# Placing seven heads' attention output by 48 small products, and the FFN's first products in two column groups, in a one-core decode layer

## The chip, the cores and the metric

The kernel runs on one core of a Trainium2 chip. The metric is the device time of one execution in microseconds. Only the core's own engines matter: TensorE (PE, with its weight loads PEld), VectorE (DVE), ScalarE (ACT), GpSimd (POOL), SyncE (SP), and the 16 DMA engines that its queues feed.

## What is computed

One token (D = 448) goes through a layer norm, and then through two branches that are added to x:

```python
xn = _layernorm(x)
# A: 16 query heads on 8 key/value heads, 65536 keys of 256 numbers each, cached in HBM
q = (xn @ wq)                                  # 448 x 4096
p = softmax(q k^T * 256 ** -0.5)               # for each head over 65536 keys
A = (p @ v).reshape(1, 4096) @ wo              # 4096 x 448
# B: a gated FFN on the same row, scaled by sigmoid(xn . w_r)
y = (silu(xn @ w_gate) * (xn @ w_up)) @ w_down # 448 x 1792, 448 x 1792, 1792 x 448
B = xn + sigmoid(xn . w_r) * y
out = x + A + B
```

All inputs are bfloat16. The key and value caches are 268 MB each; with the weights some 549 MB are read once.

## The kernel before, in words

The keys and values of one kv head are cut into four turns, 32 turns in all. One turn's keys (8 MB) land in one of two ring slots, its values (8 MB) in the third slot. In a turn PE transposes the keys (fp32 pairs of bf16) into `ps_t`, DVE and ACT copy them to `kt_all`, PE forms the scores (`k_QK`, into `ps_q`), ACT copies them out (`EVQ`), PE turns them round (`k_JT`, into `ps_s`), then come the maximum (`pe_m1t`), its broadcast (`pe_bc`), the exponentials on ACT (`EXP`), their sum (`pe_tot`, copied by DVE as `LS`), and one turn later the product with the values (`pe_V`, four column groups into `ps_o`), its transposition (`dve_ob`, `pe_oT`) into `oT_all`. Each engine runs its own list in the order in which the program writes it; a `W` is a semaphore wait of one engine, an `O` an operation that others can wait for. SP issues all large loads in one queue, in the order of the `item` calls.

The change touches the end (`ending`), which runs after the last turn's key sets. Seven of the eight heads are complete by then but for the scaling of their four turns against each other; the last head still lacks its last turn, whose values are the last large load. Before, PE and DVE worked in this order:

1. `pe_turn`: DVE scales and adds the seven heads (`head_weights`, `OTF`), PE transposes the result (`OTROW`), DVE writes it as 14 rows of 256 (`OROW`), and ACT's queue stores it to HBM (`hop 0`, tensor `o_flat`) and, once it has landed, loads it back as 128 partitions of 28 numbers (`hop 1`, tile `oT_h`). Partition p then holds the inputs 28p to 28p+27 of `wo`, whose rows lie in SBUF in the same order (`wo_rows`).
2. the last turn's maximum, `BC`, exponentials and `TOT`, and the weights of the last head.
3. `pe_ffn1`: 2 x 14 products of 448 columns for gate and up, into four PSUM banks; ACT's sigmoid (`SG`), DVE's two multiplications (`GS`, `H`); `pe_ffn_hT`: 14 small products that put the 1792 numbers on partitions (`HTP`, copied as `HTH`); `pe_ffn2`: 14 products with `w_down`.
4. `pe_attn`: 16 of the 28 columns of `oT_h` times their rows of `wo`, into one row of `ps_q`; DVE adds FFN, residual and this row (`YS`, `YX`, `SUM`).
5. `FIN_BASE` puts that sum into `ps_s` as the start of an accumulation in two column groups (`fin`: columns 0 to 207 and 208 to 447, on partitions 0 and 32). Then the last values: `pe_V` in two parts of 48 and 16 products (the program's main block ends between them), `dve_ob`, `pe_oT`, the other 12 columns of `oT_h` (`FIN_X`), the last head (`FIN`), two copies and the store of the output.

The last loads in SP's queue are the last values in two parts (6 MB and 2 MB), `wo` rows in two parts (`wx`, 896 and 448 KB) and the last head's `wo` rows in three parts (`wo_end`). These three go into a part of `kt_all` and wait for `HT`, that is for `HTH`.

Of the kernel before, what the change touches and what calls it, by code (L numbers as in the profile page):

```python
# [21 lines left out]
def bass_parallel_sum__gqa_block_cached__moe_arch_mod__decode_kernel(  # L22
# [625 lines left out]

    def pe_turn():
        W("dve", "OTSB", NU - 2)  # L650
        head_weights(0, Hkv - 1, 0, NT)
        for hf in range(NH):
            W("dve", "OW", 0, hf)
            O("dve", ("OTF", hf), lambda it, hf=hf: nc.vector.tensor_reduce(
                out=oT_f[:, hf, :, :], in_=oT_all[:, hf, 1:1 + NT, :].rearrange("p (h t) i -> p h i t", t=U), axis=AX.X, op=ALU.add))
# [12 lines left out]

    def hop(k, dst, src):
        items["oh", k] = ("oh%d" % k, 16)  # L670
        prog["act"].append(("d", here[0], ("DMA", "oh", k), (dst, src), "oh%d" % k))

    def pe_attn():
        W("pe", "DMA", ("oh", 1))
        W_item("pe", "wo")
        O("pe", "ATTN", lambda it: [mm(ps_a, lhsT=oT_h[:, f:f + 1], rhs=wo_all[:, f * D:(f + 1) * D],
                                       start=f == 0, stop=f == FR - WX - 1) for f in range(FR - WX)][-1])

    def pe_ffn1():
# [16 lines left out]

        O("pe", "FFN1G", half(0, 0))
        for c in range(2):
            W("act", "FFN1G")
            O("act", ("SG", c), lambda it, c=c: nc.scalar.activation(out=sg_sb[c], in_=ps_tf[c][0:2, 0:FB], func=ACTF.Sigmoid))  # L700
        O("pe", "FFN1", half(WGN // 2, 2))
        v = nc.vector
        for c in range(2):
            W("dve", "SG", c)
            O("dve", ("GS", c), lambda it, c=c: v.tensor_tensor(out=sg_sb[c], in0=ps_tf[c][0:2, 0:FB], in1=sg_sb[c], op=ALU.mult))
        for c in range(2):
            W("dve", "GS", c)
# [1 line left out]
            O("dve", ("H", c), lambda it, c=c: v.tensor_tensor(out=h_sb[:, c * FB:(c + 1) * FB], in0=sg_sb[c],
                                                               in1=ps_tf[2 + c][0:2, 0:FB], op=ALU.mult))  # L710

    def pe_ffn_hT():
        W("pe", "H", 0)
        W("pe", "H", 1)
        W("pe", "LS", NU - 1)

        def f(it):
            hv = h_sb.rearrange("s (p t) -> s p t", t=FK)
            for t in range(FK):
                ins = mm(ps_m[0:P // 2, C_HT + 2 * t:C_HT + 2 * t + 2], lhsT=hv[:, :, t],  # L720
                         rhs=sel_bf[0:2, 0, :], start=True, stop=True)
# [4 lines left out]
        for k in range(2):  # L726
            O("dve", ("HTH", k), lambda it, k=k: nc.vector.tensor_copy(
                out=hT_sb[k * P // 2:(k + 1) * P // 2, :],
                in_=ps_m[0:P // 2, C_HT:C_HT + 2 * FK].rearrange("p (t s) -> p s t", s=2)[:, k, :]))
# [46 lines left out]
    def ending():  # L776
# [4 lines left out]
        k_QK(n - 1)  # L781
        pe_turn()
        k_JT(n - 1)
        W("pe", "OROW")
# [4 lines left out]
        pe_tot(T)
        head_weights(Hkv - 1, Hkv, NT, NU - 1)  # L790
        for hf in range(NH):
            W("dve", "OW", Hkv - 1, hf)
            O("dve", ("OTE", hf), lambda it, hf=hf: nc.vector.tensor_reduce(
                out=oT_e[:, hf, :], in_=oT_all[:, hf, 1 + NT:NU, :].rearrange("p t i -> p i t"), axis=AX.X, op=ALU.add))
# [16 lines left out]
        O("dve", "SUM", lambda it: nc.vector.tensor_tensor(out=sum_f, in0=ps_a, in1=sum_f, op=ALU.add))
# [308 lines left out]
```

## Time and profile before

| | |
|---|---|
| median of 3 runs | 1285.49 us (1284.19 to 1285.6) |
| the profiled execution, its time | 1284.63 us |
| its span, first to last instruction | 1283.3 us |
| busy: PE, DVE, ACT | 73%, 45%, 36% of the span |
| bytes read from HBM | 549.04 MB, 428 GB/s over the span |
| mean granted TensorE clock | 0.867 |

In the rows of the timeline the first number is the start and the second the length, both in microseconds of the span; what stands in brackets is how long the engine had been idle and what released it. Each line of the table of stretches gives busy time and, after x, the number of instructions of each engine, then the granted clock (1.00 is full, 0.50 half), the share of the time that the DMA engines moved data, and GB/s. A DMA row ends in the time from issue to landing. PE's products all carry one line number, that of a helper, so they are told apart by their tiles: output, then what they read.

### The profile page before, as it was taken

To read this page: it belongs to the slowest core of one execution; us is meant where nothing else is said; L and a number is where in the kernel's file an instruction comes from. 1 tells how busy PE (TensorE), PEld (TensorE's weight loads), DVE (VectorE), ACT (ScalarE), POOL (GpSimd) and SP (SyncE) were. 2 spreads that over 40 slices of the span, in tenths; PEclk is the share of its full clock that TensorE was granted. 3 is DMA by queue.
4 is the path that set the end of the run, shared out by engine and by line. 5 is a ranking of instruction groups with operands and counts; after the bars stand their busy time and mean duration, and the time that the engine had idled before them with its cause. 6 is when DMAs were issued, how large, how long until landed. Compare 5 with 4: busy or idle time off the path is not lost. (4 is left out here: it accounts for less than half of the span.)

```text
span 1283.3 us, 23437 instructions
## 1 busy us (share of the span) xinstructions
PE 938.5 (73%) x9761; PEld 646.4 (50%) x9761; DVE 576.8 (45%) x1123; ACT 462.8 (36%) x719; POOL 8.0 (1%) x37
## 2 busy tenths in 40 slices
PE   1887877678866777876678867668766668766677
PEld 1655655445644445654455544445544445544453
DVE  2554544435543445444345444345444345444352
ACT  0543433334432334333234333334333334333330
POOL 2000000000000000000000000000000000000000
PEclk9998978888887889888789878899888889888898
DMA  9999999999999999999999999999999999999995
GB/s 408 435 439 427 433 437 435 427 435 437 435 425 437 435 435 429 433 441 429 429 437 439 427 433 435 437 427 437 435 435 427 435 437 433 429 437 439 427 425 244
DMA packets 10990, 549.19 MB, mean 428 GB/s; under 512 B 1362, under 2 KB 1764, under 8 KB 2020
## 3 DMA queue, kind: packets, MB, share of 16 engines
q1 hardware_dynamic: 10804, 549.03, 99.0%
q8 instruction: 7, 0.11, 0.0%
q10 hardware_dynamic: 176, 0.02, 0.0%
q14 instruction: 3, 0.02, 0.0%
HBM read 549.04 MB, written 0.01 MB: 428 GB/s over the span
## 5 line engine op out<-in xcount | busy, mean ns | idle before, releaser
L404 PE MATMUL ps_t<-ident_f,ring 128*128 128x128 f32 x4096 | 627.4, 298 | 311.1 <-DMA ring<-in_A_k_cache_dram 277.8
L465 DVE COPY kt_all<-ps_t 128x1024 bf16<-128x1024 bf16 x768 | 492.2, 685 | 584.0 <-PE ps_q L404 574.2
L404 PEld LDWEIGHTS ps_t<-ident_f,ring 128*128 128x128 f32 x4096 | 485.5, 151 | 472.6 <-DMA ring<-in_A_k_cache_dram 280.6
L467 ACT ACTIVATE kt_all<-ps_t 128x1024 bf16<-128x1024 bf16 x256 | 262.3, 1025 | 411.1 <-PE ps_q L404 410.8
L404 PE MATMUL ps_q<-kt_all,q_cur 128*2 128x512 bf16 x2056 | 175.3, 419 | 5.4 <-ACT s L489 5.0
L467 ACT ACT_TABLE_LOAD x32 | 41.1, 1283 | 362.7 <-PE ps_q L404 362.7
L489 ACT ACTIVATE s<-ps_q 98x512 bf16<-98x512 f32 x257 | 151.6, 590 | 1.3 <-PE ps_q L404 1.3
L404 PE MATMUL ps_o<-ring,p_sb 128*4 128x512 bf16 x2048 | 117.7, 382 | 0.3 <-PEq L1075 0.3
L404 PEld LDWEIGHTS ps_o<-ring,p_sb 128*4 128x4 bf16 x2048 | 46.0, 85 | 57.0 <-issue 3.5
L404 PEld LDWEIGHTS ps_s<-sel_bf,s 128*128 128x128 bf16 x1032 | 62.7, 98 | 3.8 <-ACT s L489 0.6
L404 PE MATMUL ps_s<-sel_bf,s 128*128 128x8 bf16 x1032 | 63.7, 167 | 0.5 <-ACT s L489 0.5
L588 DVE CAST ob_sb<-ps_o 100x512 bf16<-100x512 f32 x33 | 22.8, 691 | 90.2 <-PE ps_o L404 90.2
L404 PEld LDWEIGHTS ps_q<-kt_all,q_cur 128*2 128x2 bf16 x2056 | 26.8, 79 | 56.9 <-issue 44.4
L549 ACT ACTIVATE p_sb<-S_sb,negmax 128x128 bf16<-128x128 bf16 x66 | 26.8, 428 | 5.4 <-DVE negmax L541 5.4
L404 PEld LDWEIGHTS ps_m<-diag,ones_f 2*128 2x128 f32 x66 | 9.9, 186 | 10.3 <-DVE diag L532 10.3
L404 PE MATMUL ps_m<-diag,ones_f 2*128 2x2 f32 x66 | 12.7, 260 | 2.4 <-DVE diag L532 0.6
L520 DVE TENSOR_REDUCE m<-S_sb 128x2 f32<-128x256 bf16 x33 | 13.9, 420 | 1.1
L517 DVE CAST S_sb<-ps_s 128x256 bf16<-128x256 f32 x33 | 13.7, 415 | 0.0
L549 ACT ACTIVATION_READ_ACCUMULATOR p_sb<-S_sb,negmax 128x1 f32 x66 | 12.4, 188 | 0.0
L404 PEld LDWEIGHTS ps_m<-rowsum,ones_f 128*128 128x128 f32 x66 | 10.2, 195 | 1.3 <-DVE gm_all L543 1.3
L404 PE MATMUL ps_m<-rowsum,ones_f 128*128 128x2 f32 x66 | 9.6, 215 | 1.3 <-ACT p_sb L549 1.3
L404 PE MATMUL ps_m<-ident_f,m 128*2 128x128 f32 x33 | 9.1, 276 | 1.3 <-DVE m L520 1.3
(98 smaller groups left out, 131.5 us busy)
## 6 DMA issues: line engine op xcount, KB each, us to landing
ring<-in_A_v_cache_dram SPq DMA_DIRECT2D x1, 6144.0 KB, 22.7
ring<-in_A_wq_dram SPq DMA_DIRECT2D x1, 3584.0 KB, 11.2
ring<-in_A_v_cache_dram SPq DMA_DIRECT2D x1, 2048.0 KB, 27.3
ring<-in_A_wo_dram SPq DMA_DIRECT2D x1, 1792.0 KB, 42.6
ring<-in_B_w_gate_dram SPq DMA_DIRECT2D x1, 1568.0 KB, 32.5
ring<-in_B_w_up_dram SPq DMA_DIRECT2D x1, 1568.0 KB, 35.9
ring<-in_B_w_down_dram SPq DMA_DIRECT2D x1, 1568.0 KB
ring<-in_A_wo_dram SPq DMA_DIRECT2D x1, 896.0 KB, 29.1
```

What stands on the lines that cost most here:

```text
L404: return pe.matmul(*a, **k)
L465: O(e, ("EV", s, m), lambda it: nc.vector.tensor_copy(out=kt[:, :], in_=tb[:, :]), f"ev{m}")
L467: O(e, ("EV", s, m), lambda it: nc.scalar.activation(out=kt[:, :], in_=tb[:, :], func=ACTF.Copy), f"ev{m}")
L489: O("act", ("EVQ", s), lambda it: nc.scalar.activation(out=s2[s % 2][0:QROWS, :], in_=ps_q[0:QROWS, :], func=ACTF.Copy), "evq")
L517: O("dve", ("SCOPY", u), lambda it: nc.vector.tensor_copy(out=S_sb[:, :, :], in_=ps_sn), "sc")
L520: O("dve", ("M1", u), lambda it: nc.vector.tensor_reduce(out=m1[:, :], in_=S_sb[:, :, :].rearrange("p n i -> p i n"), axis=AX.X, op=ALU.max))
L549: O("act", ("EXP", b, i), lambda it, i=i: nc.scalar.activation(out=p_sb[:, :, i], in_=S_sb[:, :, i], func=ACTF.Exp, bias=negmax[:, i:i + 1 ...
L588: O("dve", ("OB", t), lambda it: nc.vector.tensor_copy(out=ob_sb[0:OROWS, :], in_=ps_o[0:OROWS, :]))
```

## The change

The way through HBM goes. DVE converts the seven heads' sums to bf16 (`OTG`, tile `oT_g`), and 48 products with columns of the identity matrix as weights (32 columns each, in four column groups, one to three result columns) place them in PSUM (`pe_rows`, into `ps_q`), from where DVE copies them to `oT_h` (`OTH`). For this the rows of `wo` lie in another order: partition p of a pair of kv heads holds 8 neighbouring rows of that pair, and of the seventh head 4. The first load of `wo` (two pairs, 1792 KB) so has two stretches of 7168 bytes on each partition, not one of 14336; the late ones keep theirs. The identity matrix gets a tile of its own, since its old place is overwritten by values.

`pe_ffn1` alternates its products between two column groups (partitions 0 and 32) of one bank for the gate and one for up. It moves ahead of the last turn's maximum: the new order on PE is FFN1, the 48 products, M1T, `HTP` (now into `ps_o`), BC, FFN2, TOT, `FIN_BASE`, ATTN, the last values. ATTN now adds into `ps_s` in two column groups (32 products in place of 16), behind `FIN_BASE`; the operation `SUM` is gone. On DVE `OTH` stands ahead of `GS` and `H`, and `LS` and the last head's weights behind `HTH`. On ACT the sigmoids stand ahead of the last exponentials.

```diff
-    ident_bf = slots[2][:, SLOT - P:SLOT]
+    ident_bf = S_("ident_bf", [P, P], BF16)
...
     def wo_rows(f0, f1):
-        return A_wo[0:(Hq - rep) * Dh, :].rearrange("(p f) n -> p f n", f=FR)[:, f0:f1, :].rearrange("p f n -> p (f n)")
+        r = A_wo[f0 * P:f1 * P, :]
+        if f1 <= PR * NPAIR:
+            return r.rearrange("(k p c) n -> p k (c n)", p=P, c=PR)
+        return r.rearrange("(k p c) n -> p k (c n)", k=1, p=P)
...
-        for hf in range(NH):
-            W("pe", "OTF", hf)
-            O("pe", ("OTROW", hf), ...)
-        W("dve", "OTROW", NH - 1)
-        O("dve", "OROW", ...)
-        W("act", "OROW")
-        hop(0, o_flat, o_row)
+        W("dve", "OTF", NH - 1)
+        O("dve", "OTG", lambda it: nc.vector.tensor_copy(out=oT_g[:, :, :, :], in_=oT_f[:, :, :, :]))
+
+    def pe_rows():
+        W("pe", "OTG")
+        W("pe", "EVQ", NU * SETS - 1)
+        def f(it):
+            for a in range(PR // NH):
+                for hf in range(NH):
+                    for g in range(NG):
+                        o = ps_r[32 * g:32 * g + 32, 0:PR * NPAIR].rearrange("p (k c) -> p c k", c=PR)[:, a * NH + hf, :]
+                        mm(o, lhsT=ident_bf[:, a:P:PR // NH], rhs=oT_g[:, hf, g // rep:2 * NPAIR:2, g % rep],
+                           start=True, stop=True, tile_position=(0, 32 * g))
+            ...  # 16 more for the seventh head, one result column each
+        O("pe", "OROW", f)
+        W("dve", "OROW")
+        O("dve", "OTH", lambda it: nc.vector.tensor_copy(out=oT_h[:, :], in_=ps_r))
...
     def pe_attn():
-        W("pe", "DMA", ("oh", 1))
         W_item("pe", "wo")
-        O("pe", "ATTN", ... mm(ps_a, lhsT=oT_h[:, f:f + 1], rhs=wo_all[:, f * D:(f + 1) * D], ...)
+        W("pe", "OTH")
+        O("pe", "ATTN", lambda it: [fin(wo_all, f * D, oT_h[:, f:f + 1]) for f in range(FR - WX)][-1])
...
-                    ins = mm(ps_tf[b0 + c % 2][0:2, 0:FB], ...)
+                    g = 32 * (c % 2)
+                    ins = mm(ps_tf[b0][g:g + 2, 0:FB], ..., tile_position=(0, g), skip_group_check=True)
...
-        O("pe", "FFN1", half(WGN // 2, 2))
+        O("pe", "FFN1", half(WGN // 2, 1))
+        pe_rows()
...
-        pe_turn()
+        dve_heads()
         k_JT(n - 1)
-        W("pe", "OROW")
+        pe_ffn1()
         pe_m1t(T)
+        pe_ffn_hT()
         pe_bc(T)
-        W("act", "DMA", ("oh", 0))
-        hop(1, oT_h[:, :], o_flat.rearrange("r d -> (r d)").rearrange("(p f) -> p f", f=FR))
+        pe_ffn2()
         pe_tot(T)
         head_weights(Hkv - 1, Hkv, NT, NU - 1)
...
-        pe_ffn1()
-        pe_ffn_hT()
-        pe_ffn2()
-        pe_attn()
...
-        W("dve", "ATTN")
...
-        O("dve", "SUM", lambda it: nc.vector.tensor_tensor(out=sum_f, in0=ps_a, in1=sum_f, op=ALU.add))
-        W("pe", "SUM")
+        W("pe", "YX")
         O("pe", "FIN_BASE", lambda it: fin(sum_f, 0, ones_f[0:1, 0:1], first=True))
+        pe_attn()
+        W("pe", "HT")
         pe_V(T, True)
```

More of the change, by code (lines that the diff above doesn't have):

```diff
@@ L104, in T_ @@
         temp[0] += n2
-        assert temp[0] <= SLOT - P
+        assert temp[0] <= SLOT
         return a if dtype == BF16 else a.bitcast(dtype)
@@ L130, in bass_parallel_sum__gqa_block_cached__moe_arch_mod__decode_kernel @@
     w_all = S_("w_all", [P, NU, rep], FP32)
-    wl_all = S_("wl_all", [P, NU, rep], FP32)
     gm_h = S_("gm_h", [P, Hkv, rep], FP32)
@@ L138, in bass_parallel_sum__gqa_block_cached__moe_arch_mod__decode_kernel @@
     oT_f = S_("oT_f", [P, NH, Hkv - 1, rep], FP32)
+    oT_g = S_("oT_g", [P, NH, Hkv - 1, rep], BF16)
     oT_h = S_("oT_h", [P, FR], BF16)
-    o_flat = nc.dram_tensor("o_flat", [(Hkv - 1) * rep, Dh], BF16).ap()
     KB = 2 * FB
-    sg_sb = [kt_all[0:2, c * KB:(c + 1) * KB].bitcast(FP32) for c in range(2)]
+    sg_sb = [kt_all[32 * c:32 * c + 2, 0:KB].bitcast(FP32) for c in range(2)]
     h_sb = kt_all[0:2, 2 * KB:3 * KB]
@@ L146, in bass_parallel_sum__gqa_block_cached__moe_arch_mod__decode_kernel @@
     res_bf = kt_all[0:1, 3 * KB + 2 * D:3 * KB + 3 * D]
-    o_row = kt_all[0:(Hkv - 1) * rep, 3 * KB:3 * KB + Dh]
-    assert Dh <= KB and WON <= 2 * KB and 3 * KB + 3 * D <= NKT * 8 * P
+    assert WON <= 2 * KB and 3 * KB + 3 * D <= NKT * 8 * P
     hT_sb = S_("hT_sb", [P, FK], BF16)
@@ L166, in bass_parallel_sum__gqa_block_cached__moe_arch_mod__decode_kernel @@
     ps_q = PS_("ps_q", [P, 512], FP32)
-    ps_a = ps_q[0:1, 0:D]
+    ps_r = ps_q[:, 0:FR]
     ps_s = PS_("ps_s", [P, 512], FP32)
@@ L172, in bass_parallel_sum__gqa_block_cached__moe_arch_mod__decode_kernel @@
     C_XNT, C_BC, C_TOT, C_OT, C_Q, C_BIG = 0, 16, 18, 22, 28, 64
-    C_HT = C_Q
-    assert C_Q + NH * Hq + 4 <= C_BIG and C_HT + 2 * FK <= C_BIG and C_BIG + NH * P <= 512
+    assert C_Q + NH * Hq + 4 <= C_BIG and C_BIG + NH * P <= 512
     sems = {}
@@ L183, in SEM @@
         return name
-    for n_ in ["pe", "act", "dve", "pool", "qk", "jt", "evq", "exp", "pc", "qc", "sc", "w0", "out", "res", "wq", "wg", "wo", "wd", "we0", "we1", "we2", "wx0", "wx1", "oh0", "oh1", "pv"]:
+    for n_ in ["pe", "act", "dve", "pool", "qk", "jt", "evq", "exp", "pc", "qc", "sc", "w0", "out", "res", "wq", "wg", "wo", "wd", "we0", "we1", "we2", "wx0", "wx1", "pv"]:
         SEM(n_)
@@ L272, in wo_view, with wo_place @@
         return t.rearrange("p (i f n) -> p i f n", i=rep, f=NH)
+    PR = P * 2 * rep * Dh // P // P
+    NPAIR = (Hkv - 1) // 2
+    assert PR * NPAIR + rep * Dh // P == FR and (Hkv - 1) % 2 == 1
     def wo_rows(f0, f1):
-        return A_wo[0:(Hq - rep) * Dh, :].rearrange("(p f) n -> p f n", f=FR)[:, f0:f1, :].rearrange("p f n -> p (f n)")
+        r = A_wo[f0 * P:f1 * P, :]
+        if f1 <= PR * NPAIR:
+            assert f0 % PR == 0 and f1 % PR == 0
+            return r.rearrange("(k p c) n -> p k (c n)", p=P, c=PR)
+        assert f0 == PR * NPAIR and f1 == FR
+        return r.rearrange("(k p c) n -> p k (c n)", k=1, p=P)
+    def wo_place(f0, f1):
+        n = 1 if f1 > PR * NPAIR else (f1 - f0) // PR
+        return wo_all[:, f0 * D:f1 * D].rearrange("p (k x) -> p k x", k=n)
     def k_item(u):
@@ L290, in bass_parallel_sum__gqa_block_cached__moe_arch_mod__decode_kernel @@
     item("wd", [(wd_area, flat_src(B_w_down, FK * D), "wd"), (x_again, A_x[0], "wd")])
-    item("wo", [(wo_all[:, 0:(FR - WX) * D], wo_rows(0, FR - WX), "wo")])
+    item("wo", [(wo_place(0, FR - WX), wo_rows(0, FR - WX), "wo")])
     slot_item("v", NU - 1, 2, [("last%d" % k, J) for k, J in enumerate(LAST)], [("VFREE", NU - 2)])
@@ L295, in bass_parallel_sum__gqa_block_cached__moe_arch_mod__decode_kernel @@
         f0, f1 = LATE_AT[k:k + 2]
-        item(("wx", k), [(wo_all[:, f0 * D:f1 * D], wo_rows(f0, f1), "wx%d" % k)])
+        item(("wx", k), [(wo_place(f0, f1), wo_rows(f0, f1), "wx%d" % k)])
     ENDS = [(0, 0, NH), (1, 0, 1), (1, 1, NH)]
@@ L627, in head_weights @@
         ls = heads(l_all[:, 1 + n0:1 + n1, :])
-        w, wl = heads(w_all[:, n0:n1, :]), heads(wl_all[:, n0:n1, :])
+        w = heads(w_all[:, n0:n1, :])
         W("dve", "GM", h1 * U - 1)
@@ L636, in head_weights @@
         W("dve", "LS", h1 * U - 1)
-        O("dve", ("WL", h0), lambda it: v.tensor_tensor(out=wl, in0=w, in1=ls, op=ALU.mult))
+        O("dve", ("WL", h0), lambda it: v.tensor_tensor(out=ls, in0=w, in1=ls, op=ALU.mult))
         W("dve", "WL", h0)
-        O("dve", ("LH", h0), lambda it: v.tensor_reduce(out=l_h[:, h0:h1, :], in_=wl.rearrange("p h t i -> p h i t"), axis=AX.X, op=ALU.add))
+        O("dve", ("LH", h0), lambda it: v.tensor_reduce(out=l_h[:, h0:h1, :], in_=ls.rearrange("p h t i -> p h i t"), axis=AX.X, op=ALU.add))
         W("dve", "LH", h0)
@@ L647, in head_weights, with dve_heads @@
                 out=oT_all[:, hf, 1 + a:1 + b, :], in0=oT_all[:, hf, 1 + a:1 + b, :], in1=w_all[:, a:b, :], op=ALU.mult))
-    def pe_turn():
+    def dve_heads():
         W("dve", "OTSB", NU - 2)
@@ L655, in pe_turn @@
                 out=oT_f[:, hf, :, :], in_=oT_all[:, hf, 1:1 + NT, :].rearrange("p (h t) i -> p h i t", t=U), axis=AX.X, op=ALU.add))
-        HR = (Hkv - 1) * rep
-        for hf in range(NH):
-            W("pe", "OTF", hf)
-            O("pe", ("OTROW", hf), lambda it, hf=hf: mm(ps_m[0:HR, C_BIG + hf * P:C_BIG + (hf + 1) * P],
-                                                        lhsT=oT_f[:, hf, :, :].rearrange("p h i -> p (h i)"), rhs=ident_f[:, :],
-                                                        is_transpose=True, start=True, stop=True))
@@ L663, in pe_turn @@
-        W("dve", "OTROW", NH - 1)
-        O("dve", "OROW", lambda it: nc.vector.tensor_copy(
-            out=o_row.rearrange("r (p f) -> r f p", f=NH), in_=ps_m[0:HR, C_BIG:C_BIG + NH * P].rearrange("r (f p) -> r f p", f=NH)))
-        W("act", "OROW")
-        hop(0, o_flat, o_row)
-    def hop(k, dst, src):
-        items["oh", k] = ("oh%d" % k, 16)
-        prog["act"].append(("d", here[0], ("DMA", "oh", k), (dst, src), "oh%d" % k))
+        W("dve", "OTF", NH - 1)
+        O("dve", "OTG", lambda it: nc.vector.tensor_copy(out=oT_g[:, :, :, :], in_=oT_f[:, :, :, :]))
@@ new lines, in pe_rows @@
+    def pe_rows():
[8 more added lines that the diff above has]
+                           start=True, stop=True, tile_position=(0, 32 * g))
+            for a in range(PR // NH // 2):
+                for hf in range(NH):
+                    for g in range(NG):
+                        c = PR * NPAIR + a * NH + hf
+                        n = PR // NH // 2
+                        b0 = a + 32 * n * (g % 2)
+                        ins = mm(ps_r[32 * g:32 * g + 32, c:c + 1], lhsT=ident_bf[:, b0:b0 + 31 * n + 1:n],
+                                 rhs=oT_g[:, hf, 2 * NPAIR, g // 2:g // 2 + 1], start=True, stop=True, tile_position=(0, 32 * g))
+            return ins
+        O("pe", "OROW", f)
+        W("dve", "OROW")
+        O("dve", "OTH", lambda it: nc.vector.tensor_copy(out=oT_h[:, :], in_=ps_r))
@@ L673, in pe_attn @@
     def pe_attn():
-        W("pe", "DMA", ("oh", 1))
         W_item("pe", "wo")
-        O("pe", "ATTN", lambda it: [mm(ps_a, lhsT=oT_h[:, f:f + 1], rhs=wo_all[:, f * D:(f + 1) * D],
-                                       start=f == 0, stop=f == FR - WX - 1) for f in range(FR - WX)][-1])
+        W("pe", "OTH")
+        O("pe", "ATTN", lambda it: [fin(wo_all, f * D, oT_h[:, f:f + 1]) for f in range(FR - WX)][-1])
     def pe_ffn1():
@@ L690, in f @@
                     o = base + rr * F + c * FB
-                    ins = mm(ps_tf[b0 + c % 2][0:2, 0:FB], lhsT=xnT_sb[:, x0:x0 + 2], rhs=wg_area[:, o:o + FB],
-                             start=c % 2 not in seen, stop=n >= len(todo) - 2)
+                    g = 32 * (c % 2)
+                    ins = mm(ps_tf[b0][g:g + 2, 0:FB], lhsT=xnT_sb[:, x0:x0 + 2], rhs=wg_area[:, o:o + FB],
+                             start=c % 2 not in seen, stop=n >= len(todo) - 2, tile_position=(0, g), skip_group_check=True)
                     seen.add(c % 2)
@@ L699, in pe_ffn1 @@
             W("act", "FFN1G")
-            O("act", ("SG", c), lambda it, c=c: nc.scalar.activation(out=sg_sb[c], in_=ps_tf[c][0:2, 0:FB], func=ACTF.Sigmoid))
-        O("pe", "FFN1", half(WGN // 2, 2))
+            O("act", ("SG", c), lambda it, c=c: nc.scalar.activation(out=sg_sb[c], in_=ps_tf[0][32 * c:32 * c + 2, 0:FB], func=ACTF.Sigmoid))
+        O("pe", "FFN1", half(WGN // 2, 1))
+        pe_rows()
         v = nc.vector
@@ L704, in pe_ffn1 @@
             W("dve", "SG", c)
-            O("dve", ("GS", c), lambda it, c=c: v.tensor_tensor(out=sg_sb[c], in0=ps_tf[c][0:2, 0:FB], in1=sg_sb[c], op=ALU.mult))
+            O("dve", ("GS", c), lambda it, c=c: v.tensor_tensor(out=sg_sb[c], in0=ps_tf[0][32 * c:32 * c + 2, 0:FB], in1=sg_sb[c], op=ALU.mult))
         for c in range(2):
@@ L709, in pe_ffn1 @@
             O("dve", ("H", c), lambda it, c=c: v.tensor_tensor(out=h_sb[:, c * FB:(c + 1) * FB], in0=sg_sb[c],
-                                                               in1=ps_tf[2 + c][0:2, 0:FB], op=ALU.mult))
+                                                               in1=ps_tf[1][32 * c:32 * c + 2, 0:FB], op=ALU.mult))
     def pe_ffn_hT():
@@ L714, in pe_ffn_hT @@
         W("pe", "H", 1)
-        W("pe", "LS", NU - 1)
+        W("pe", "OB", NU - 2)
         def f(it):
@@ L719, in f @@
             for t in range(FK):
-                ins = mm(ps_m[0:P // 2, C_HT + 2 * t:C_HT + 2 * t + 2], lhsT=hv[:, :, t],
+                ins = mm(ps_o[0:P // 2, 2 * t:2 * t + 2], lhsT=hv[:, :, t],
                          rhs=sel_bf[0:2, 0, :], start=True, stop=True)
@@ L728, in pe_ffn_hT @@
                 out=hT_sb[k * P // 2:(k + 1) * P // 2, :],
-                in_=ps_m[0:P // 2, C_HT:C_HT + 2 * FK].rearrange("p (t s) -> p s t", s=2)[:, k, :]))
+                in_=ps_o[0:P // 2, 0:2 * FK].rearrange("p (t s) -> p s t", s=2)[:, k, :]))
         alias("dve", "HT")
@@ L809, in ending @@
         O("dve", "YX", lambda it: nc.vector.tensor_tensor(out=sum_f, in0=sum_f, in1=x_again, op=ALU.add))
-        W("dve", "YX")
-        O("dve", "SUM", lambda it: nc.vector.tensor_tensor(out=sum_f, in0=ps_a, in1=sum_f, op=ALU.add))
-        W("pe", "SUM")
+        W("pe", "YX")
         W("pe", "SCOPY", T)
         O("pe", "FIN_BASE", lambda it: fin(sum_f, 0, ones_f[0:1, 0:1], first=True))
+        pe_attn()
+        W("pe", "HT")
         pe_V(T, True)
```

## The prediction

> **What bounds the kernel now.** I read the page's totals first, then DMA, clock and PE in stretches of the end, then the DMA issues, then the timeline from 1240 us on. The page's totals:
>
> ```profile
> span 1283.3 us, 23437 instructions
> HBM read 549.04 MB, written 0.01 MB: 428 GB/s over the span
> ```
>
> The end in stretches of 3.41 us, cut where the granted clock changes:
>
> ```profile
> 1242.39:1245.81 3.42, 1.15 (x21) 0.47 (x19) 2.15 (x8) 1.42 (x4) 0.00 (x0) 0.99 1.08 461
> 1245.81:1249.22 3.41, 1.05 (x7) 0.58 (x7) 2.19 (x10) 0.00 (x0) 0.00 (x0) 0.50 1.07 462
> ...
> 1259.46:1262.88 3.42, 1.76 (x14) 1.70 (x14) 1.41 (x4) 0.00 (x0) 0.00 (x0) 0.99 0.83 346
> 1262.88:1266.29 3.41, 3.21 (x9) 1.12 (x10) 0.44 (x2) 0.00 (x0) 0.00 (x0) 0.51 0.98 409
> ...
> 1269.70:1273.12 3.42, 1.18 (x8) 0.26 (x6) 1.90 (x3) 0.00 (x0) 0.00 (x0) 0.99 0.26 93
> 1273.12:1276.53 3.41, 3.41 (x34) 1.09 (x36) 0.00 (x0) 0.00 (x0) 0.00 (x0) 0.51 0.00 0
> 1276.53:1279.94 3.41, 2.27 (x42) 0.78 (x35) 0.69 (x1) 0.00 (x0) 0.00 (x0) 1.00 0.00 0
> 1279.94:1283.30 3.36, 1.80 (x35) 1.48 (x32) 0.69 (x3) 0.36 (x1) 0.00 (x0) 1.00 0.02 5
> ```
>
> The loads bound the kernel up to some 1271 us: DMA is busy throughout. Then it moves nothing for 12 us, while PE still has the last values to do. So the end hangs on PE's list, not on a load. The landings say how much sooner it could be:
>
> ```profile
> ring<-in_A_v_cache_dram SPq DMA_DIRECT2D x1, 6144.0 KB, 22.7
> ring<-in_A_v_cache_dram SPq DMA_DIRECT2D x1, 2048.0 KB, 27.3
> ring<-in_B_w_up_dram SPq DMA_DIRECT2D x1, 1568.0 KB, 35.9
> kt_all<-in_A_wo_dram SPq DMA_DIRECT2D x2, 112.0 KB, 8.3
> ```
>
> ```profile
> 1204.18 0.43 SPq L888 DMA_DIRECT2D ring<-in_B_w_up_dram  x1
> 1239.92 0.80 SPq L888 DMA_DIRECT2D ring<-in_A_v_cache_dram  x2
> 1262.96 1.28 SPq L888 DMA_DIRECT2D kt_all<-in_A_wo_dram  x3
> ```
>
> The last values land at 1239.9 + 22.7 = 1262.6 and about 1267.6, the last of `wo_end` (issued third, near 1263.8) at about 1272.0. The kernel starts on the values only at 1273.26. Why, the timeline says (PE, DVE and ACT of the end):
>
> ```profile
> 1244.38 0.60 ACT L489 ACTIVATE s<-ps_q 98x512 bf16<-98x512 f32 x1 [1.31 <-PE ps_q L404]
> ...
> 1246.43 0.33 DVE L654 TENSOR_REDUCE oT_f<-oT_all 128x14 f32<-128x56 f32 x2
> ...
> 1247.08 0.29 PE L404 MATMUL ps_s<-sel_bf,s 128*128 128x8 bf16 x4
> ...
> 1249.66 0.58 PE L404 MATMUL ps_m<-diag,ones_f 2*128 2x2 f32 x2 [0.62 <-DVE diag L532]
> ...
> 1251.99 7.40 PE L404 MATMUL ps_t<-ring,xnT_sb 128*2 128x448 bf16 x28
> ...
> 1255.66 0.21 ACT L634 ACTIVATE w_all<-w_all 128x8 f32<-128x8 f32 x1 [4.31 <-DMA o_flat<-kt_all]
> ...
> 1256.90 0.23 DVE L793 TENSOR_REDUCE oT_e<-oT_all 128x2 f32<-128x6 f32 x2
> ...
> 1259.50 1.14 DVE L709 TENSOR_TENSOR kt_all<-kt_all,ps_t 2x448 bf16<-2x448 f32 x2 [0.60 <-PE ps_t L404]
> ...
> 1260.78 1.76 PE L404 MATMUL ps_m<-sel_bf,kt_all 2*64 2x2 bf16 x14 [1.39 <-DVE kt_all L709]
> ...
> 1263.08 4.33 PE L404 MATMUL ps_t<-ring,hT_sb 128*1 128x448 bf16 x14 [0.54 <-DVE hT_sb L727]
> ...
> 1267.25 3.19 PE L404 MATMUL ps_q<-ring,oT_h 128*1 128x448 bf16 x16
> 1270.65 0.67 DVE L806 SCALAR_TENSOR_TENSOR kt_all<-ps_t,stat,ring 1x448 f32<-1x448 f32 x1 [7.30 <-PE ps_q L404]
> ...
> 1272.67 0.66 PE L404 MATMUL ps_s<-kt_all,ones_f 1*1 1x208 f32 x4 [2.24 <-DVE kt_all L811]
> ...
> 1273.26 4.31 PE L404 MATMUL ps_o<-ring,p_sb 128*4 128x512 bf16 x48
> ...
> 1279.93 1.29 PE L404 MATMUL ps_s<-ring,oT_h 128*1 128x208 bf16 x23
> ```
>
> One chain: FFN1, HTP, FFN2, ATTN, DVE's sums, FIN_BASE, values. Whatever starts that chain sooner or shortens it moves the end one for one, until it meets the last landing.
>
> **The change part by part.** Times are those of this execution.
>
> FFN1's start. It waited behind OTROW, the maximum and TOT, but its weights had landed at 1204.2 + 35.9 = 1240.1. Now only the last JT stands ahead, which needs the copy of the scores (ends 1244.98); with 0.3 us for its four products (the row at 1247.08) FFN1 starts at 1245.35, 6.6 us sooner.
>
> FFN1's length. Two column groups were not used for this; the nearest row is the FIN_X one at 1279.93: 23 products of 208 and 240 columns in two groups at full clock in 1.29 us, 0.056 us each, so 0.112 for 448 columns, 3.1 us for 28. At half clock twice that. The clock: after a stretch with PE busy for 1.15 or 1.76 us of 3.4 the next ran at half, after 2.27 us at full. The stretch before 1245.81 would hold 1.15 + 0.3 + 0.46 = 1.9 us, between the two; I take half clock, nearest to 1.76. Then 4 products before 1245.81, 15 to 17 in the next stretch, the rest at full: 4.65 us (bounds 3.1, and 7.4 if the groups don't overlap), end at 1250.0.
>
> The Trainium skill ("TensorE: Matmul & The Clock Gate", rules for kernels) has the clock fall only when PE idles for about 3 us. By it FFN1 would stay at full clock and take 3.1 us, and the sum would be 1.5 us lower. The trace disagrees as to the rule: PE was busy for 1.76 us of the stretch from 1259.46, with no idle time over 1.4 us, and fell to 0.51.
>
> The 48 products. Nothing like them is in the end. Below, the setup's query products; above, HTP, 1.76 us for 14, 0.126 each, with 64 strided weight columns:
>
> ```profile
> 13.95 3.13 PE L404 MATMUL ps_m<-xnT_sb,ring 128*128 128x2 bf16 x112
> ```
>
> That is 0.028 each. So 1.3 to 6.0 us. I take 0.045, since a load here has half of HTP's weight columns and PE keeps four groups apart as in the values' products: 2.2 us, end at 1252.2. Their input `oT_g` is ready at about 1247.0 (OTF ends at 1246.76), well ahead.
>
> The same skill page puts a weight load at its columns over 1.2 GHz, 27 ns for 32; "TensorEngine Tiling" (restrictions) adds that column tiling forgoes the fast load. By these 48 cost an estimated 1.3 us, and the sum would be 0.9 lower.
>
> OTH, GS, H. DVE is in order: OTH waits for the 48 products, and GS, ready since the sigmoids (about 1248.5), is queued behind it. Before, GS hid under FFN1's second half and only H (1.14) followed. Now OTH 0.25, GS 1.14 (the size of H's row) and H 1.14 stand in a row: H ends at 1254.8, HTP starts at 1254.95. From FFN1's end to HTP: 1.39 before, 4.95 now, 3.6 lost. GMAX and DIAG follow on DVE, under HTP.
>
> HTP to FFN2. HTP 1.76 as before, to 1256.7; BC (0.58) now stands between it and FFN2, beside HTH, so FFN2 starts at 1257.3. The gap was 0.54: nothing gained. FFN2: half clock to 1259.46, then full, 3.7 us against 4.33; it ends at 1261.0.
>
> Tail of the sums. TOT is queued on PE behind FFN2, and LS with the whole last head's weights behind TOT on DVE, ahead of YS. TOT 0.35; LS, maximum, difference, the exponential (0.21 in its row), then the run that ended at 1257.13 (1.23 us from ACT's end at 1255.87): 2.1 together; XN_AGAIN 0.4; YS and YX 1.35. FIN_BASE starts at 1265.25. Before, FFN2's end to FIN_BASE took 5.26 (ATTN 3.19, YS, YX, SUM); now 4.25.
>
> ATTN stands behind FIN_BASE (0.66): 32 products of 224 columns at half clock, 0.112 each, 3.6 us, to 1269.5 (1.8 at full clock).
>
> The values. 1269.5 is past both landings. PE has then been dense since 1265.3, so the clock is full from 1269.70, where before it was half up to 1276.53:
>
> ```profile
> 1159.71 2.76 PE L404 MATMUL ps_o<-ring,p_sb 128*4 128x512 bf16 x48
> ```
>
> So 0.2 + 2.76, to 1272.3, against 4.31. From there to the span's end 5.73 us (1277.57 to 1283.3), unchanged.
>
> Costed at nothing: the hop's two DMAs (off PE's chain, ATTN started long after; its ACT wait of 4.31 us delayed only the last head's weights); the second table load on ACT, 1.28 us at most between sigmoid and EXP, hidden under DVE's GS and H, which end 6 us after the sigmoids; without that cover it would delay EXP, then TOT. `wo`'s shorter stretches ride under the DMA bound: a tenth of their 4.2 us (1.8 MB at 428 GB/s) would be 0.4 us on a queue with 4 us to spare. SP issues `wo_end` at 1257 in place of 1263, in the same place behind the same loads; it lands no later.
>
> Sum: the values start at 1269.5 in place of 1273.26 (3.8), and run 1.5 faster: 5.3. Span 1278.0; with the 1.33 us outside it 1279.3, rounded up to 1279.4. That execution was 0.86 under the median of the runs (1285.49).
>
> **The rivals.** First, the loads take over. If the clock stays full in FFN1 (1.5), FFN2 (1.1) and ATTN (1.8) and the products cost 0.028 (0.9), the chain ends before `wo_end` lands at 1272.0; then come two last products (0.3) and the 1.55 us from FIN's end to the span's: span 1273.9, time 1275.2, a floor. Some of these together are likely, since the clock's stretches need not fall alike in each execution. The skill's idle rule alone, FFN1 at full clock, gives 1277.9.
>
> Second, the 48 products cost what HTP's do: 6.0 us, 1283.2. For it: their weights are strided too.
>
> Third, column groups of two share one bank and don't overlap: FFN1 7.4, time 1282.1. Against it: the FIN_X row does overlap in `ps_s`, one bank.
>
> Fourth, the other side: each placement waits for the one before to drain, as four groups write one bank with new weights each time. The bound is a pair alone, 0.58 us for two at half clock in the BC row, 0.29 each: 13.9 us, 11.7 over, time 1291. It decides from 0.045 + 6.1/48 = 0.17 us a product on: there nothing is left of the gain. Against it: the values' products alternate four groups in `ps_o` at 0.057 us.
>
> **How the numbers follow.** The chain as summed, 1277 to 1281.5: 0.60. Loads take over, 1275.2 to 1277: 0.17. HTP's price, 1282 to 1284: 0.11. No overlap, about 1282: 0.05. No pipelining, above 1285: 0.07. What this kernel's timing can tell from no change is 0.2%, 2.6 us: faster is below 1282.9, slower above 1288.1. Faster: 0.60 + 0.17 + 0.05 + half of 0.11 = 0.87; the other half, same, 0.06; slower 0.07. The range goes from the floor to HTP's price, 1275.2 to 1283.3, and leaves out about 0.13.
>
> **What would show it.** FFN1 starting at 1245.3 and lasting 3.1 to 4.7; the 48 products in about 2.2, with DVE's wait for them and GS right behind; YX after TOT; the values starting near 1269.5 with DMA done by 1271; `wo_end` not waited for. Wrong if the values start after 1273, if FIN waits for `wo_end`, or if FFN1 waits for its weights.

## The result, and the profile after

The changed kernel takes 1278.16 us (median of 6 runs, 1276.59 to 1279.64) against 1285.41 (6 runs): ratio 0.9944, 95% interval 0.9931 to 0.9957, 7.25 us faster. The profiled execution took 1278.87 us with a span of 1277.6.

The table of stretches of the changed kernel, cut where its steps begin (columns as before):

```profile
1246.65:1249.82 3.17, 3.17 (x80) 1.82 (x77) 2.34 (x11) 2.80 (x4) 0.00 (x0) 1.00 1.11 475
1249.82:1252.68 2.86, 0.21 (x2) 0.01 (x1) 2.63 (x6) 0.75 (x1) 0.00 (x0) 1.00 0.95 412
1252.68:1255.01 2.33, 2.27 (x16) 2.22 (x17) 0.74 (x4) 0.00 (x0) 0.00 (x0) 0.55 1.02 429
1255.01:1260.10 5.09, 5.09 (x15) 1.66 (x15) 0.23 (x2) 0.88 (x4) 0.00 (x0) 0.54 1.01 436
1260.10:1264.12 4.02, 0.35 (x3) 0.26 (x3) 3.06 (x14) 0.21 (x1) 0.00 (x0) 0.88 0.83 355
1264.12:1268.10 3.98, 3.98 (x41) 2.81 (x45) 0.00 (x0) 0.00 (x0) 0.00 (x0) 0.50 0.96 402
1268.10:1271.82 3.72, 3.72 (x50) 2.15 (x39) 0.00 (x0) 0.00 (x0) 0.00 (x0) 0.75 0.73 274
...
1272.00:1277.60 5.60, 3.02 (x52) 1.99 (x52) 1.38 (x4) 0.36 (x1) 0.00 (x0) 1.00 0.00 0
```

From the top: FFN1 with the 48 products; DVE's OTH, GS, H with PE idle; HTP and BC; FFN2; TOT and DVE's sums with PE idle again; FIN_BASE and ATTN; the last values; the rest. DMA now stands still for under 6 us at the end where it was 12. The timeline of the same end:

```profile
1245.81 0.60 ACT L498 ACTIVATE s<-ps_q 98x512 bf16<-98x512 f32 x1 [1.31 <-PE ps_q L413]
...
1246.65 2.44 PE L413 MATMUL ps_t<-ring,xnT_sb 128*2 128x448 bf16 x24
...
1249.11 0.71 PE L413 MATMUL ps_q<-oT_g,ident_bf 128*32 128x3 bf16 x44
1249.29 1.28 ACT L558 ACT_TABLE_LOAD   x1
...
1249.93 0.19 DVE L691 CAST oT_h<-ps_q 128x28 bf16<-128x28 f32 x1 [0.74 <-PE ps_q L413]
1250.03 1.25 DVE L726 TENSOR_TENSOR kt_all<-ps_t,kt_all 2x448 f32<-2x448 f32 x2
1251.31 1.25 DVE L730 TENSOR_TENSOR kt_all<-kt_all,ps_t 2x448 bf16<-2x448 f32 x2
...
1252.71 1.76 PE L413 MATMUL ps_o<-sel_bf,kt_all 2*64 2x2 bf16 x14 [2.68 <-DVE kt_all L730]
...
1255.01 5.12 PE L413 MATMUL ps_t<-ring,hT_sb 128*1 128x448 bf16 x14
...
1260.48 0.16 DVE L567 COPY l_all<-ps_m 128x2 f32<-128x2 f32 x1 [5.24 <-PE ps_m L413]
...
1264.12 0.96 PE L413 MATMUL ps_s<-kt_all,ones_f 1*1 1x208 f32 x4 [3.67 <-DVE kt_all L825]
...
1265.01 2.96 PE L413 MATMUL ps_s<-ring,oT_h 128*1 128x208 bf16 x30
...
1268.16 3.65 PE L413 MATMUL ps_o<-ring,p_sb 128*4 128x512 bf16 x43
```

FFN1 and the 48 products are done 3.2 us after FFN1's start, which follows the last JT at once. DVE stands idle for 5.24 us until `LS` gets TOT, which is queued on PE behind FFN2. The values start near 1268, where it was 1273.26, and nothing in the end waits for a load.

### The profile page after: what moved, and what is told of

It is laid out like the page before. It is cut to its first block, busy times and chain, and to the rows that moved or that the text cites. A ratio compares the mean times of both kernels' runs of the same rounds, so it can differ in the third digit from the quotient of the medians.

```text
span 1277.6 us, 23557 instructions
## 1 busy us (share of the span) xinstructions
PE 942.5 (74%) x9823; PEld 654.9 (51%) x9823; DVE 576.8 (45%) x1123; ACT 463.8 (36%) x720; POOL 8.0 (1%) x37
## 5 line engine op out<-in xcount | busy, mean ns | idle before, releaser
L413 PE MATMUL ps_t<-ident_f,ring 128*128 128x128 f32 x4096 | 635.5, 300 | 304.1 <-DMA ring<-in_A_k_cache_dram 272.8
L413 PEld LDWEIGHTS ps_t<-ident_f,ring 128*128 128x128 f32 x4096 | 492.4, 153 | 465.9 <-DMA ring<-in_A_k_cache_dram 275.6
```

Source lines behind the costliest of these rows:

```text
L413: return pe.matmul(*a, **k)
```

## The experiments

Each is an edit of the changed kernel. Medians in us, ratio to the kernel before with its 95% interval, and the difference of the median from the changed kernel's 1278.16. The kernel before was run again beside each group: 1285.52 beside the first four, 1284.88 beside TOT inside, ATTN ahead, idle products and the three moves, 1285.28 beside the other two. So the differences carry some 0.5 us of drift; by the ratios TOT inside, ATTN ahead and idle products gain about 2 us each, not 2.5 to 2.8, and the three moves 1.0.

| edit | median | ratio | difference |
|---|---|---|---|
| FFN1 in one column group | 1280.54 | 0.9961 [0.9948, 0.9975] | +2.4 |
| FFN1 late | 1281.29 | 0.9971 [0.9959, 0.9983] | +3.1 |
| the hop kept | 1282.24 | 0.9980 [0.9968, 0.9992] | +4.1 |
| the 48 products twice | 1279.14 | 0.9952 [0.9939, 0.9966] | +1.0 |
| OTH behind GS and H | 1276.98 | 0.9935 [0.9921, 0.9948] | -1.2 |
| TOT inside FFN2 | 1275.68 | 0.9929 [0.9915, 0.9942] | -2.5 |
| ATTN ahead of FIN_BASE | 1275.37 | 0.9930 [0.9917, 0.9944] | -2.8 |
| idle products to keep the clock | 1275.53 | 0.9927 [0.9913, 0.9941] | -2.6 |
| the last three moves without idle products | 1276.42 | 0.9936 [0.9923, 0.9950] | -1.7 |
| the same with idle products at the end | 1275.67 | 0.9927 [0.9914, 0.9941] | -2.5 |

**FFN1 in one column group.**

```diff
-  mm(ps_tf[b0][g:g + 2, 0:FB], ..., tile_position=(0, g), ...)
+  mm(ps_tf[b0 + c % 2][0:2, 0:FB], ...)
```

> FFN1 without column groups (four banks, partition 0, as before), all else as after. Theory A, the chain through PE and DVE sets the end one for one: 28 products at 0.187 us at full clock take 5.2 us in place of 2.5, so the end moves by about +2.7 us, to some 1280.9, and the stretch from the issue of the last values' load to the span's end grows from 36.3 to 39.0 us. If half the products fall to half clock, up to +4. Rival B, the loads already set the end: no change, 1278.2.

+2.4. FFN1's first 26 products took 5.08 us where 24 had taken 2.44; the chain behind it moved with it:

```profile
1245.30 5.08 PE L413 MATMUL ps_t<-ring,xnT_sb 128*2 128x448 bf16 x26
```

**FFN1 late.**

```diff
-  pe_ffn1(); pe_m1t(T); pe_ffn_hT(); pe_bc(T); pe_ffn2(); pe_tot(T); head_weights(...)
+  pe_m1t(T); pe_bc(T); pe_tot(T); head_weights(...); pe_ffn1(); pe_ffn_hT(); pe_ffn2()
```

> FFN1, the 48 products, HTP and FFN2 back behind the last turn's maximum, BC, TOT and the last head's weights, with column groups and the 48 products kept. Theory A: FFN1 starts some 6 us later; FFN2's end is followed by YS at once, since TOT and LS lie ahead, which gives 2.4 back: +3.6 us, 1281.8, stretch 39.9. Rival, the order is worth nothing beside the hop's removal and the column groups: +0 to 0.5.

+3.1, and the timeline shows both parts of it: FFN1 starts at 1251.25, and FIN_BASE follows FFN2's end by 1.5 us, since TOT and `LS` lie ahead:

```profile
1251.25 4.27 PE L413 MATMUL ps_t<-ring,xnT_sb 128*2 128x448 bf16 x24
...
1261.46 4.66 PE L413 MATMUL ps_t<-ring,hT_sb 128*1 128x448 bf16 x14 [0.55 <-DVE hT_sb L748]
...
1267.59 0.57 PE L413 MATMUL ps_s<-kt_all,ones_f 1*1 1x208 f32 x4 [1.48 <-DVE kt_all L825]
```

**The hop kept.** Transposes and store stand behind FFN1, the load behind the last exponentials; the rows of `wo` have their old order.

```diff
-  O("pe", "OROW", f)   # 48 products
+  O("pe", ("OTROW", hf), ...); O("dve", "OROW", ...); hop(0, o_flat, o_row)   # behind FFN1
...
   pe_bc(T)
+  W("act", "DMA", ("oh", 0)); hop(1, oT_h[:, :], ...)
```

> The trip through HBM kept (transposes and store behind FFN1, load behind the last exponentials on ACT's queue, old order of wo rows), FFN1 early and in column groups. The prediction priced the hop's removal at nothing. Theory A: with the early FFN1 that no longer holds: store 7.5 us and load 11.1 us as in the profile of before end near 1269, ATTN wanted them at 1265.0, so +4 us, 1282.2, stretch 40.4. Rival, the hop is still hidden: no change, 1278.2.

+4.1 in the median, with a wide scatter (11 runs from 1280.0 to 1286.87), and here ATTN waits for the load:

```profile
1251.03 0.34 ACTq L892 DMA_DIRECT2D o_flat<-kt_all  x1
...
1258.53 0.36 ACTq L892 DMA_DIRECT2D oT_h<-o_flat  x1
...
1264.70 0.96 PE L408 MATMUL ps_s<-kt_all,ones_f 1*1 1x208 f32 x4 [3.68 <-DVE kt_all L813]
...
1268.32 2.96 PE L408 MATMUL ps_s<-ring,oT_h 128*1 128x208 bf16 x30 [2.66 <-DMA oT_h<-o_flat]
```

In the profile of before, the hop's load was issued at 1255.25 and took 11.1 us, and ATTN started at 1267.25 behind FFN2 without waiting for it. So the hop was hidden as long as ATTN came late, and the products alone should be worth nothing to the old order (not run). The 4 us hold for the hop as it was placed here. Its store was issued 5.55 us behind the copied scores, where it was 2.81 in before; the 2.74 us between are about as long as ATTN's wait. A hop started ahead of FFN1, which would make FFN1 wait for DVE, was not tried.

**The 48 products twice.**

```diff
+  for again in range(2):
       for a in range(PR // NH): ...
```

> The 48 products issued twice. Theory A: they lie on the path and cost 0.02 us each as the profile of after has it: +0.9 us, 1279.1, stretch 37.2. Rival, they cost what HTP's do, 0.126 each: +6, 1284. Rival B, hidden: no change.

The median moved by 1.0, but the ranges of the runs overlap (1278.75 to 1280.71 against 1276.59 to 1279.64), so the time alone settles only that 6 us is out. The trace gives the price: 92 of them where there were 44, in 1.11 us against 0.71, and HTP starts 6.46 us after FFN1 (1252.88 less 1246.42) against 6.06. That is 0.40 us for 48, 0.008 each:

```profile
1246.42 2.43 PE L413 MATMUL ps_t<-ring,xnT_sb 128*2 128x448 bf16 x24
...
1248.88 1.11 PE L413 MATMUL ps_q<-oT_g,ident_bf 128*32 128x3 bf16 x92
...
1252.88 1.76 PE L413 MATMUL ps_o<-sel_bf,kt_all 2*64 2x2 bf16 x14 [2.68 <-DVE kt_all L731]
```

**OTH behind GS and H.**

```diff
-  pe_rows()   # inside pe_ffn1, ahead of GS and H on DVE
...
   pe_ffn1()
+  pe_rows()
   pe_m1t(T)
```

> OTH behind GS and H on DVE, all else as after. Theory A, the prediction's term of GS queued behind OTH: from FFN1's start to HTP's 5.1 us in place of 6.06, -0.9 us if nothing gives it back, 1277.3. Rival, FFN2 and ATTN only meet the half clock elsewhere: no change within 0.5 us.

-1.2 in the median; the ranges overlap (1276.09 to 1277.81). The wait did go, but this profiled execution doesn't show the 5.1 us: FFN1 ran partly at half clock in it, its first 24 products in 4.12 us, not 2.44. HTP starts 6.0 us after FFN1:

```profile
1245.02 4.12 PE L413 MATMUL ps_t<-ring,xnT_sb 128*2 128x448 bf16 x24
...
1249.62 1.25 DVE L729 TENSOR_TENSOR kt_all<-kt_all,ps_t 2x448 bf16<-2x448 f32 x2 [0.19 <-PE ps_t L413]
...
1251.02 1.76 PE L413 MATMUL ps_o<-sel_bf,kt_all 2*64 2x2 bf16 x14 [0.94 <-DVE kt_all L729]
```

The 5.1 us are in the kernel of the three moves below (FFN1 at 1246.43, HTP at 1251.57).

**TOT inside FFN2.**

```diff
-  pe_ffn2(); pe_tot(T)
+  FFN2 products 0 to 5; pe_tot(T); FFN2 products 6 to 13
```

> TOT placed between the sixth and the seventh product of FFN2, so that LS and the last head's weights run under FFN2 and YS follows its end. Theory A, the prediction's term of 2.1 us for LS and the weights behind TOT lies on the path: from FFN2's end to FIN_BASE 1.5 us in place of 4.0, the end moves by -2.3 us, to 1275.9, stretch from the last values' issue to the span's end 34.0 in place of 36.3. Rival, the sooner start only moves ATTN and the values into a stretch of half clock: -1.0. Rival B, loads bind: no change.

-2.5. YS follows FFN2, FIN_BASE starts at 1259.84, and the values are so early that PE waits for loads:

```profile
1259.84 0.63 PE L413 MATMUL ps_s<-kt_all,ones_f 1*1 1x208 f32 x4 [1.74 <-DVE kt_all L830]
...
1268.10 1.03 PE L413 MATMUL ps_o<-ring,p_sb 128*4 128x512 bf16 x16 [1.75 <-DMA ring<-in_A_v_cache_dram]
```

So the chain gave more than the end shows: the rest stopped at the loads, and behind this wait the clock was at half again (the 23 products of FIN_X took 2.23 us, 1.29 in the changed kernel).

**ATTN ahead of FIN_BASE.**

```diff
-  W("pe", "YX"); FIN_BASE (first=True); pe_attn()
+  pe_attn() (first at f == 0); W("pe", "YX"); FIN_BASE
```

> ATTN ahead of FIN_BASE, in PE's wait for DVE's sums (it starts the accumulation, FIN_BASE adds to it). Theory A: the 3.0 us of ATTN leave the path, and PE is not idle for 3.7 us, so the values run at full clock: -3.0 to -3.5 us, to about 1275, where the last landing of wo_end (1272.0) plus 1.9 us is the floor. Rival, ATTN only changes places with the wait: -0.5 at most.

-2.8, at the floor. ATTN runs at full clock in 1.80 us in the wait for DVE's sums, the values follow FIN_BASE, and the last thing PE waits for is `wo_end`:

```profile
1258.88 1.80 PE L413 MATMUL ps_s<-ring,oT_h 128*1 128x208 bf16 x32
...
1263.13 2.76 PE L413 MATMUL ps_o<-ring,p_sb 128*4 128x512 bf16 x48
...
1272.04 0.08 PEld L413 LDWEIGHTS ps_s<-kt_all,oT_sb 128*1 128x1 bf16 x2 [0.21 <-DMA kt_all<-in_A_wo_dram]
```

The span of this execution was 1273.9, the floor that the prediction had worked out; two of the five runs took 1276.38 and 1276.84. Of the kernels run it has the lowest median, but four lie within 0.3 us and can't be told apart.

**Idle products to keep the clock.** Nothing of the kernel's own work changes; the added products' result is not used.

```diff
   pe_m1t(T)
+  11 products of 448 columns into an unused bank
   pe_ffn_hT()
...
+  16 products of 448 columns into an unused bank
   W("pe", "YX")
```

> After, with products that serve nothing put in PE's two idle times (11 of 448 columns behind M1T, 16 behind TOT, into an unused bank). Theory A, the clock is granted by how busy PE was in the stretch before: FFN2 takes 2.6 us in place of 5.1 and ATTN and the values 2 us less, the end comes to the floor, about -3.3 us, 1275. Rival, the light HTP products alone lower the clock: FFN2 stays at 5 us, the time 0 to +0.5.

-2.6. With PE busy in those two gaps FFN2 and ATTN run at full clock:

```profile
1253.71 2.81 PE L413 MATMUL ps_t<-ring,hT_sb 128*1 128x448 bf16 x14 [0.24 <-DVE hT_sb L748]
...
1261.01 1.80 PE L413 MATMUL ps_s<-ring,oT_h 128*1 128x208 bf16 x32
```

FFN2 took 2.81 us against 5.12, ATTN 1.80 against 2.96 for 30 of its 32. The clock in its stretches of HTP and of FFN2:

```profile
1251.30:1253.50 2.20, 2.06 (x16) 1.99 (x16) 0.76 (x4) 0.00 (x0) 0.00 (x0) 1.00 1.13 477
1253.50:1256.70 3.20, 2.99 (x16) 1.37 (x16) 0.29 (x3) 0.88 (x4) 0.00 (x0) 1.00 0.89 384
```

The light HTP products stood in the same place, so it wasn't they alone that lowered the clock. At the end PE waited 2.15 us for the second part of the values, and FIN_X ran at half clock here too (2.36 us).

**The three moves, without and with idle products at the end.**

```diff
   TOT inside FFN2; ATTN ahead of FIN_BASE; OTH behind GS and H
```

> TOT inside FFN2, ATTN ahead of FIN_BASE, and OTH behind GS and H on DVE, all three. Theory A: the chain alone would give -2.3 - 3.0 - 0.7 = -6.0 us, so the loads take over: FIN waits for the last part of wo_end, span about 1274.0 with an issue of the last values at 1241.3, that is a stretch of 32.7, time near 1274.8. Rival, no floor: stretch 30.3, time 1272.2.

It did not come to the floor: 1276.42, 1.0 above ATTN's move alone. PE waited 2.14 us for the second part of the values and ran what follows at half clock:

```profile
1267.46 1.03 PE L413 MATMUL ps_o<-ring,p_sb 128*4 128x512 bf16 x16 [2.14 <-DMA ring<-in_A_v_cache_dram]
...
1269.95 2.36 PE L413 MATMUL ps_s<-ring,oT_h 128*1 128x208 bf16 x23 [0.41 <-DMA ring<-in_A_wo_dram]
```

The second kernel puts 10 products without use into that wait:

```diff
   the last values, part 1
+  10 products of 448 columns into an unused bank
   the last values, part 2
```

> The three moves, and 10 products that serve nothing (448 columns, unused bank) between the two parts of the last values, in PE's wait of 2.1 us for the second part. Theory A: the three moves alone ended at 1274.8 behind loads that had landed by 1272.0 because PE had idled and ran FIN_X and FIN at half clock (2.36 us in place of 1.29): now FIN_X takes 1.3, FIN waits for wo_end, span about 1273.9, time 1275.2. Rival, the loads themselves were later in that kernel: no change, 1276.4.

1275.67, 0.75 us lower, span 1274.3. The granted clock in the stretch of FIN_X and FIN, without and with (one line of each kernel's table of stretches):

```profile
1269.90:1273.40 3.50, 3.30 (x32) 2.56 (x32) 0.15 (x2) 0.11 (x1) 0.00 (x0) 0.55 0.23 83
```

```profile
1269.90:1273.40 3.50, 2.47 (x36) 1.36 (x36) 0.69 (x3) 0.36 (x1) 0.00 (x0) 1.00 0.27 98
```

With idle products FIN_X began 0.28 us later (1270.23 against 1269.95), and FIN still ended 0.53 us sooner (1272.73 against 1273.26), behind a last wait for `wo_end`:

```profile
1270.23 1.67 PE L413 MATMUL ps_s<-ring,oT_h 128*1 128x208 bf16 x24 [0.15 <-DMA ring<-in_A_wo_dram]
```

So in these two executions the clock, not later loads, held the three moves back. The rest of 0.5 us above the expected 1275.2 is about what the landing of `wo_end` differs between executions (it was last waited for until 1272.46 there, until 1272.04 with ATTN's move). Not every wait lowered the clock: in this last kernel PE also waited 2.27 us for the first part of the values, and its 48 products took the 2.76 us of full clock:

```profile
1263.02 2.76 PE L413 MATMUL ps_o<-ring,p_sb 128*4 128x512 bf16 x48 [2.27 <-DMA ring<-in_A_v_cache_dram]
```

## Why the prediction was right, step by step

The forecast was 1279.4 and the mechanism held: one chain through PE and DVE, no load in the way, faster by the start and the length of FFN1. Three steps were undone one at a time, and each put the end back, by 2.4, 3.1 and 4.1 us. Together these are more than 7.25, since they aren't independent: without the early FFN1 the hop is hidden again, as in the profile of before.

Within the sum, sizes were off in both directions and partly cancelled, so that the time came within 1.3 us is in part luck. From the copied scores to the end of the span the sum had 33.05 us, the profiled execution took 31.19: FFN1 and the 48 products were 3.68 us shorter than summed, FFN2 and the values 2.3 us longer. And the last turn, ahead of all this, ended 1.43 us later:

- The start. Predicted 0.37 us behind the copied scores, measured 0.24 (1246.41 to 1246.65). But the last turn itself ended 1.43 later in this execution (its scores were copied at 1246.41 against 1244.98), a scatter that the sum had no term for.
- FFN1 and the 48 products, 4.65 + 2.2 = 6.85 predicted, 3.17 measured: the largest miss, in two parts of 1.84 us each. FFN1 took 2.81 us (its last products end at 1249.46). The clock stayed full in the profiled execution, which the prediction had taken at half; in the kernel with OTH moved it fell, and 24 products took 4.12. Here the stretches before fit the prediction's rule, near its edge: PE was busy for 2.30 of the 3.41 us from 1242.67 in this execution, and for 1.92 of the 3.42 us from 1241.87 in that one; the prediction had 1.9. And the products added 0.36 us behind FFN1's end, 0.008 each, not 0.045: the lower bound, 0.028 from the setup's products, was no bound, and the estimate of 1.3 us beside it was too high as well. The setup's products had no column groups; whether that is why was not tried.
- OTH, GS and H in a row behind the products: 2.75 predicted, 2.89 measured.
- HTP to FFN2's start 2.35, measured 2.30, BC between them as forecast.
- FFN2 3.7 predicted, 5.09 measured: half clock nearly to its end. The change of the clock was expected after 2.2 us and came after some 4.7, by the mean of 0.54. For FFN1 it was enough that the stretches fall elsewhere in each execution. For FFN2 and the values the rule itself failed, by which a stretch with PE busy for 2.27 us is followed by full clock. These are stretches of the changed kernel, cut where its clock can change (columns as before):

```profile
1252.91:1256.32 3.41, 3.38 (x20) 2.46 (x20) 0.77 (x5) 0.88 (x4) 0.00 (x0) 0.50 1.00 423
1256.32:1259.73 3.41, 3.41 (x10) 1.16 (x9) 0.00 (x0) 0.00 (x0) 0.00 (x0) 0.50 0.97 418
...
1263.15:1266.56 3.41, 2.44 (x22) 1.46 (x24) 0.88 (x2) 0.00 (x0) 0.00 (x0) 0.50 0.95 403
1266.56:1269.97 3.41, 3.41 (x41) 2.50 (x40) 0.00 (x0) 0.00 (x0) 0.00 (x0) 0.50 0.98 392
```

  And these are two of the kernel before, in the first of which PE has FFN2 alone:

```profile
1262.79:1266.20 3.41, 3.12 (x9) 1.12 (x10) 0.53 (x2) 0.00 (x0) 0.00 (x0) 0.50 1.00 418
1266.20:1269.62 3.42, 3.42 (x20) 1.51 (x18) 0.00 (x0) 0.00 (x0) 0.00 (x0) 1.00 0.97 383
```

  HTP, BC and the start of FFN2 kept PE busy for 3.38 us, FIN_BASE and part of ATTN for 2.44, and the next stretch was at half both times; 3.12 us of FFN2 alone were followed by full clock. So PE's busy time alone doesn't tell the clock. That the small products of HTP and BC count for less would fit, but was not tried by itself.
- FFN2's end to FIN_BASE 4.25, measured 4.02. TOT's place behind FFN2 cost what was said: with TOT inside, FFN2's end to FIN_BASE (1258.1 to 1259.84) is 1.74 by the trace.
- FIN_BASE and ATTN 4.25 predicted, 3.98 measured. The values 2.8 in the sum (1269.5 to 1272.3; its own terms, 0.2 + 2.76, make 2.96), 3.72 measured, half clock again for half of it (0.75 in the mean). From there to the end 5.73, measured 5.78.

The rivals: HTP's price and no pipelining fell with the doubled products. Groups that don't overlap fell with FFN1 in one group. The loads that take over did not, in this kernel; they do, at 1275.4 to 1275.7, as soon as any one of three edits (TOT inside, ATTN ahead, idle products) has shortened the chain. PE then waits for the second part of the values in all three; FIN waits for `wo_end`, by which the prediction had worked out its floor, only with ATTN's move.

What was costed at nothing: the second table load (1249.29, 1.28 us) ended at 1250.57, and EXP waited until 1255.21 for the maximum, so its cover was ample. The hop's removal was nothing for the old order by the profile of before; the sum should have said that the early FFN1 takes that cover away, 4.1 us as the hop was placed. The new order of `wo` rows was not tried by itself; the hop's kernel had the old order, and in it the first part of `wo_end`, last but two in the queue, landed at 1255.77 + 16.1 = 1271.9, here at 1254.89 + 16.6 = 1271.5 (issue and time to landing).

The clock: the Trainium skill ("TensorE: Matmul & The Clock Gate", "Why this matters for your kernels") lets it fall when PE idles for more than about 3 us. Here PE was idle for 2.68 us before HTP and the clock was 0.55 in the stretch from 1252.68. With the gap filled it stayed at 1.00. So shorter gaps can be enough here, and the measurement decides; but they aren't always, as the 2.27 us in the last kernel show. Neither the length of a gap nor PE's busy time alone tells the clock in these runs, and the rule stays open.

## What to carry to other kernels

When the last load lands long before the end, look for the one chain behind it, and cost every edit by where it moves the start of that chain; a transfer that was hidden is hidden only until its reader comes earlier. Products queued in order carry more than their own time: a small sum behind a long product (TOT behind FFN2) cost 2.3 us of DVE work that could have run under it. After a chain has become shorter than the loads, PE's waits can lower its clock, and the last products then pay for it.

## What the runs showed of the hardware that was not expected

- Products of 128 x 32 weights and 1 to 3 columns in four column groups cost 0.008 us each when 48 more follow (0.40 us), 0.016 in the first lot (44 in 0.71, in part beside FFN1's last products). The Trainium skill ("TensorE: Matmul & The Clock Gate", "Wait — 56ns, not 53.3ns?") gives a floor of about 25 ns from start to start. No floor of that size shows here, where four groups alternate.
- HTP, 14 products with 64 strided weight columns from two partitions, took 1.76 us at a granted clock of 0.99 (before), 0.55 (after) and 1.00 (idle products). So the array's clock doesn't set its 0.126 us each.
- Three idle gaps of 2.1 to 3.7 us on PE (before HTP, before FIN_BASE, before the second part of the values) were followed by half clock, and idle products in the first two brought 2.6 us although they do nothing. A wait of 2.27 us was not followed by half clock (three moves with idle products), and of two waits for the second part of the values one of 1.75 us was (TOT inside) and one of 1.74 us was not (ATTN's move).
- GS and H take 1.25 us with one of their halves on partition 32, against 1.13 with FFN1 in one group, all on partitions 0 and 1.
